# Attention, top-1 experts and a softplus layer on one core: where buffers are zeroed, in how many pieces squares are made, in which order VectorE leaves the attention, and which engine makes the last x

## The chip, the cores and the metric

The program runs on one core of one Trainium2 chip. The metric is the device time of one execution in microseconds (us); the time before is the median of three runs. A profiled execution has a time of its own, and its trace is what the rows below come from. Engines are named as in the profile: PE is TensorE, DVE is VectorE, ACT is ScalarE, POOL is GpSimd, and SP is SyncE, which only issues DMAs here.

## The reference

Three stages follow one another; the output of each is the input of the next.

```python
# 1 attention with random features: 4 batches, 8 heads, 576 positions, 64 wide, 128 features
proj = einsum('bhsd,md->bhsm', x * scale, omega)          # x is q or k
phi = exp(proj - sum(x*x)/2 - max) / sqrt(m)
kv = einsum('bhsm,bhsd->bhmd', k_p, v);  z = k_p.sum(2)
x = einsum('bhsm,bhmd->bhsd', q_p, kv) / (einsum('bhsm,bhm->bhs', q_p, z) + 1e-6)
# 2 top-1 of 8 experts: 2304 tokens, 512 wide, hidden 1024
e = argmax(x @ w_gate);  gate = softmax(x @ w_gate)[e]
x = gate * (relu(x @ w1[e]) @ w2[e])
# 3 a layer for all tokens: 512 -> 2048 -> 512
out = softplus(x @ w_in) @ w_out
```

## The kernel before

**Attention.** It is cut into 20 items. The four batches are two pairs; of each pair five items of k are followed by five of q. An item is two position tiles of 128 of all eight heads (one tile where two rests of 64 rows are put together). So items 0 to 4 are k of the first pair, 5 to 9 its q, 10 to 14 k of the second pair, 15 to 19 its q. One loop runs over n; a step has four slots, and an item passes through it in stages, so that in one step the next item is projected (L510 to L514, each fp32 product in three parts), an item of k is summed up into kv or an item of q is transposed and multiplied (L617, L634), and the item before that is routed. `at(n, slot, ...)` hangs single pieces of work on a slot.

**What each engine does for an item.** POOL makes the sum of squares of the next item in `squares` (L454 the products, L457 the halving sums, then three small ones); DVE takes maxima (L532, L529) and the exponent's bias `nb` (L533); ACT makes the exponentials (L535). For q, DVE makes the reciprocal of the denominator `rc` (L658), the gate logits (L662) and x itself (L666: numerator times reciprocal). The x of an item goes into a tile `xt`, of which there are two in turn, and SP stores it to `x_tok` in memory (L719, L725 where an item is two rests). So the first L666 of an item waits until the store of the item two before it has landed. The two last items, 18 and 19, are the `tail`: their x stays in a tile `own` as well, and is multiplied with the gate by ACT and DVE (L714, L715).

**What lies between.** `clear_y` (L300) lets SP write zeroes, from one tile of SBUF, over a part of `x_tok` (five transfers, 1.0 MB) and over `y_comp` (twenty, 4.7 MB). Experts' weights pass a ring of 16 slots as units: a raw unit is loaded (L237), rounded by ACT (`round_raw`, L247), and DVE keeps the rest (`rest_of_raw`, L252). Units 0, 1 and 4 are loaded while the attention runs. In the passage to the experts, `first_tail` brings the first expert's block together: the gathered rows are multiplied through diagonal matrices that POOL makes (L784, L787), the tail's rows come through one-hot matrices (L767, L770), ACT and DVE split the result (L791, L792), and the first matmuls of the expert (L966 to L968) read it. `places` (from L1103, `key`) works out on DVE where each expert's tokens stand; its first operation takes a buffer whose last users it waits for, among them the stores of `own`.

**What sets the order.** Within an engine the order is the one that a scheduler chooses from its own estimate of times, written code being the preference; `behind(a, b)` fixes that a comes after b. All SP's transfers leave in SP's order, on one queue.

Of the kernel before, what the change touches and what calls it, by code (L numbers as in the profile page):

```python
# [10 lines left out]
F32 = mybir.dt.float32  # L11
# [18 lines left out]
def tile_favor_moe_softplus(  # L30
# [210 lines left out]
            reason="the transfer waits for its turn")  # L241
        return raw

    latest, first_raw = {}, []

    def round_raw(i, raw, last):
        ins = nc.scalar.activation(ring[i % NRING][:, 0:1024], raw, AF.Copy)  # L247
# [41 lines left out]
    with ExitStack() as actx:  # L289
# [157 lines left out]
        def squares(it):  # L447
            src = xin[it.bp, it.kind][it.r // 4][:, :, it.r % 4:it.r % 4 + it.nr, :]
            x2 = wk.tile([P, H, it.nr, D], F32, tag="x2", bufs=1, name="x2")
            if it is items[0]:  # L450
                for h in range(0, H, 4):
                    nc.scalar.activation(x2[:, h:h + 4], src[:, h:h + 4], AF.Square)
            else:
                nc.gpsimd.tensor_tensor(x2, src, src, op=ALU.mult)  # L454
                n = D // 2
                while n:
                    nc.gpsimd.tensor_tensor(x2[:, :, :, 0:n], x2[:, :, :, 0:n], x2[:, :, :, n:2 * n],  # L457
                                            op=ALU.add)
                    n //= 2
                it.sq = sm.tile([P, H, it.nr], F32, tag="sq", bufs=4, name="sq")  # L460
                up = sm.tile([P, H, it.nr], F32, tag="up", bufs=2, name="up")
                whole = x2[:, :, :, 0]
                nc.gpsimd.tensor_scalar(it.sq, whole, 0.5 * SCALE * SCALE, None, op0=ALU.mult)
                nc.gpsimd.tensor_scalar(up, it.sq, LNM, None, op0=ALU.add)
                nc.gpsimd.tensor_tensor(it.sq, up, it.sq, op=ALU.subtract)
            it.x2 = x2
# [157 lines left out]
        def q_product(it, grp):  # L624
# [35 lines left out]
            for g, lo, hi in parts:  # L660
                m = hi - lo
                nc.vector.tensor_tensor(  # L662
                    it.lgp[lo:hi, ii, :, h0:h1].rearrange("p i e h -> p h i e"),
                    cols(g, lo, hi, CG[g], E),
                    rcn[lo:hi].to_broadcast([m, nh, it.nr, E]), op=ALU.mult)
                nc.vector.tensor_tensor(  # L666
                    it.xt[lo:hi, ii, h0:h1, :].rearrange("p i h d -> p h i d"),
                    cols(g, lo, hi, CX[g], D),
                    rcn[lo:hi].to_broadcast([m, nh, it.nr, D]), op=ALU.mult)
# [34 lines left out]
        def route_gate(it):  # L704
            n = it.nr
            ex = sm.tile([P, 2, E], F32, tag="ex", name="ex")[:, 0:n]
            nc.scalar.activation(ex, it.dl, AF.Exp)
            gw = it.xg[:, 0:n, DM]
            nc.vector.tensor_reduce(gw, ex, axis=AX.X, op=ALU.add)
            nc.vector.tensor_scalar(gw, gw, 1e-9, None, op0=ALU.add)  # L710
            nc.vector.reciprocal(gw, gw)
            for i, t in enumerate(it.tiles if it in tail else ()):
                x, g = it.xg[:, i, 0:DM], it.xg[:, i, DM:DM + 1]
                nc.scalar.activation(tail_h[t], x, AF.Copy, scale=g)  # L714
                nc.vector.scalar_tensor_tensor(tail_l[t], x, g, tail_h[t].bitcast(F32),  # L715
                                               op0=ALU.mult, op1=ALU.subtract)
            if n == 2:
                t0 = (2 * it.bp + it.r // 4) * S
                nc.sync.dma_start(  # L719
                    x_tok[t0:t0 + 512, :].rearrange("(p r) d -> p r d", r=4)[  # L720
                        :, it.r % 4:it.r % 4 + 2, :], it.xg)
            else:
                for g in range(2):
                    t0 = (2 * it.bp + g) * S
                    nc.sync.dma_start(x_tok[t0 + 512:t0 + S, :], it.xg[g * 64:(g + 1) * 64, 0, :])  # L725
# [48 lines left out]
        def first_split():  # L774
# [15 lines left out]
            for kk in range(KD):  # L790
                nc.scalar.activation(xh[:, kk, 0:n], tp[kk][:, 0:n], AF.Copy)  # L791
                latest["DVE"] = nc.vector.tensor_tensor(  # L792
                    xl[:, kk, 0:n], tp[kk][:, 0:n], xh[:, kk, 0:n].bitcast(F32), op=ALU.subtract)
            for args in first_raw:
                rest_of_raw(*args)
            return xh, xl

        def route_rank(it):
# [64 lines left out]
        for n in range(NI + 2):  # L863
# [46 lines left out]
                loads(1)  # L910
            if n == 2:
                clear_ids(it.started)
            if n == 12:
                clear_y(it.started)
            if n == 10:
                loads_q(1)
            for i in UNITS_AT.get(n, ()):
                raw = load_raw(i, it.started)
                if i:
                    at(NI, 3, round_raw, i, raw, True)  # L920
                    first_raw.append((i, raw, True))
                else:
                    at(NI - 5, 0, round_raw, i, raw, True)
                    at(NI - 5, 1, rest_of_raw, i, raw, False)
            if n == NI - 2:

                a, b = (inp.tile([P, VO], F32, tag="kf", bufs=2, name="tail") for _ in range(2))
# [172 lines left out]
    def places():  # L1100

        key = tb.tile([P, E], F32, tag="over", name="key")
        nc.vector.scalar_tensor_tensor(key, cntb, float(E), iota_e, op0=ALU.mult,  # L1103
                                       op1=ALU.subtract)

        def rows(a):
            return a.rearrange("p (o e) -> p o e", o=1).to_broadcast([P, R, R])
# [16 lines left out]
        nc.vector.tensor_reduce(cntp[:, 1:E], more, axis=AX.X, op=ALU.add)  # L1124

        off = tb.tile([P, E + 1], F32, tag="off", name="off")
        nc.vector.memset(off[:, E:E + 1], float(NT))
        mc = tb.tile([P, E], F32, tag="nwin", name="mc")
        nc.vector.tensor_tensor(mc, cntp, caps, op=ALU.min)
        for e in reversed(range(E)):  # L1130
# [286 lines left out]
```

## Time and profile before

| | us |
|---|---|
| median of three runs | 845.51 (845.38 to 845.65) |
| the profiled execution | 852.04 |
| its span on the core | 850.3 |
| mean granted clock | 0.991 |
| PE busy | 823.5 |
| DVE, ACT, POOL busy | 490.9, 475.9, 222.5 |

The profiled execution is 6.5 us longer than the median, and 1.7 us of its time lie outside the span. The attention takes the first 185 us or so, the passage lies at 182 to 207 us, the experts and the last layer follow. A strip of the page has 40 slices of 21.3 us each, so that a strip shows in which tenth of the time an engine has gaps; the gaps themselves are read in the order in time.

### The profile page before, as it was taken

The page shows a single profiled execution, that of the slowest core. Times are in us where ns is not written, and L with a number is a line of the kernel's source. Part 1 is how long each engine was busy: PE and PEld are TensorE (multiplying, and loading weights), DVE is VectorE, ACT ScalarE, POOL GpSimd, SP SyncE. Part 2 cuts the span into 40 slices and gives each one's busy share as a digit, 9 for nine tenths or more (in the row PEclk, how much of TensorE's full clock was granted, in tenths as well). Part 3 has the DMA queues.
Part 4 walks back from the last instruction along what each step waited for, and adds up shares of the span by engine and source line. Part 5 has one row for each costly group of instructions (what it writes and reads, how often), then busy time and mean ns, then how long its engine had stood idle before and what let it go on. Part 6 is the DMA issues. An engine that isn't in the chain of part 4 may idle for free.

```text
span 850.3 us, 14078 instructions
## 1 busy us (share of the span) xinstructions
PE 823.5 (97%) x5127; PEld 763.8 (90%) x5129; DVE 490.9 (58%) x1056; ACT 475.9 (56%) x1053; POOL 222.5 (26%) x361
## 2 busy tenths in 40 slices
PE   8998998998999999999999999999999999999995
PEld 6897998987999999999999999999999999999994
DVE  6678976786787677777678666542232223222221
ACT  4686757763564455566555655565455446445442
POOL 6886889223111011101035333211001001001001
PEclk9999998999999999999999999999999999999998
DMA  9962277024896888889853321030001000000001
GB/s 224 225 180 68 72 156 242 26 69 109 263 292 214 267 255 245 278 253 306 277 185 101 124 79 45 1 112 38 1 5 70 1 1 38 1 0 38 1 1 39
DMA packets 83307, 104.21 MB, mean 123 GB/s; under 512 B 16904, under 2 KB 62632, under 8 KB 83234
## 3 DMA queue, kind: packets, MB, share of 16 engines
q1 hardware_dynamic: 79442, 93.35, 36.8%
q0 software_dynamic: 3792, 9.92, 3.5%
q8 instruction: 42, 0.69, 0.4%
q14 instruction: 31, 0.25, 0.1%
HBM read 78.68 MB, written 24.58 MB: 121 GB/s over the span
## 4 chain that ended last, share of the span: by engine, by line
PE 49%; issue 35%; DMA 7%; DVE 3%; POOL 3%; ACT 2%; SPq 1%; POOLq 0%; ACTq 0%; DVEq 0%
PE a L966 6%; PE a L968 6%; PE a L967 6%; PE y L967 4%; PE y L968 4%; PE y L966 4%; PE nm L634 4%; DMA raw<-in_moe_w_dram 2%; PE kvacc L564 2%; PE o L1253 2%; PE o L1251 2%; PE o L1248 2%; POOL out_dram L1268 2%; DMA y_comp<-w 2%; PE tq L617 2%
## 5 line engine op out<-in xcount | busy, mean ns | idle before, releaser
L1236 DVE SCALAR_TENSOR_TENSOR ab<-a,ab 128x384 f32<-128x384 f32 x96 | 53.4, 556 | 161.8 <-ACT ab L1235 151.1
L966 PE MATMUL a<-yh,w 128*128 128x384 f32 x384 | 129.6, 337 | 0.0
L968 PE MATMUL a<-yh,w 128*128 128x384 f32 x384 | 129.5, 337 | 0.0
L967 PE MATMUL a<-yl,w 128*128 128x384 f32 x384 | 129.0, 336 | 0.0
L1253 PE MATMUL o<-w,gl 128*128 128x512 f32 x288 | 114.0, 397 | 0.0
L1251 PE MATMUL o<-w,gh 128*128 128x512 f32 x288 | 113.9, 396 | 0.0
L1248 PE MATMUL o<-w,gh 128*128 128x512 f32 x288 | 112.9, 393 | 0.1
L1233 ACT ACTIVATE ab<-a 128x384 f32<-128x384 f32 x96 | 47.1, 491 | 113.0 <-PE a L968 112.9
L269 DVE TENSOR_TENSOR w<-raw,w 128x1024 fp32r<-128x1024 f32 x69 | 84.2, 1222 | 26.6 <-ACT w L266 25.9
L535 ACT ACTIVATE ph<-pj,nb 128x128 f32<-128x128 f32 x288 | 82.2, 395 | 30.0 <-DVE nb L533 21.0
L266 ACT ACTIVATE w<-raw 128x1024 fp32r<-128x1024 f32 x69 | 72.8, 1057 | 37.6 <-DMA raw<-in_moe_w_dram 37.3
L1268 POOL DMA_INDIRECT out_dram<-ob,idx x18 | 17.6, 976 | 280.7 <-ACT ob L1266 277.2
L1240 DVE TENSOR_TENSOR gl<-ab,gh 128x384 fp32r<-128x384 f32 x96 | 60.6, 631 | 52.1 <-ACT gh L1239 52.1
L1239 ACT ACTIVATE gh<-ab 128x384 fp32r<-128x384 f32 x96 | 50.4, 525 | 54.0 <-DVE ab L1236 53.7
L967 PE MATMUL y<-hl,w 128*128 128x344 f32 (+6 forms) x256 | 78.7, 308 | 0.0
L968 PE MATMUL y<-hh,w 128*128 128x344 f32 (+6 forms) x256 | 78.1, 306 | 0.0
L966 PE MATMUL y<-hh,w 128*128 128x344 f32 (+6 forms) x256 | 75.8, 306 | 1.4 <-ACT hh L1041 1.4
L967 PEld LDWEIGHTS a<-yl,w 128*128 128x128 f32 x384 | 72.4, 189 | 4.2
L966 PEld LDWEIGHTS a<-yh,w 128*128 128x128 f32 x384 | 72.2, 188 | 4.4 <-DVE ab L1236 0.2
L968 PEld LDWEIGHTS a<-yh,w 128*128 128x128 f32 x384 | 72.0, 188 | 0.0
L966 PE MATMUL a<-xh,w 128*128 128x344 f32 (+6 forms) x224 | 69.1, 309 | 0.3 <-DVE hl L1042 0.3
L968 PE MATMUL a<-xh,w 128*128 128x344 f32 (+6 forms) x224 | 67.7, 302 | 0.0
(231 smaller groups left out, 1879.6 us busy)
## 6 DMA issues: line engine op xcount, KB each, us to landing
raw<-in_moe_w_dram SPq DMA_DIRECT2D x64, 512.0 KB
raw<-in_moe_w_in_dram SPq DMA_DIRECT2D x16, 512.0 KB
raw<-in_moe_w_out_dram SPq DMA_DIRECT2D x16, 512.0 KB
yb<-y_comp SPq DMA_DIRECT2D x6, 768.0 KB
vf<-in_v_dram SPq DMA_DIRECT2D x4, 1024.0 KB
qf<-in_q_dram SPq DMA_DIRECT2D x4, 1024.0 KB
y_comp<-w SPq DMA_DIRECT2D x16, 256.0 KB
wi_f<-cvr SPq DMA_DIRECT2D x16, 256.0 KB
```

What stands on the lines that cost most here:

```text
L266: ins = nc.scalar.activation(slot[:, c:c + 1024], raw[:, c:c + 1024], AF.Copy)
L269: nc.vector.tensor_tensor(slot[:, 1024 + c:1024 + c + 1024], raw[:, c:c + 1024], slot[:, c:c + 1024].bitcast(F32), op=ALU.subtract)
L535: ins = nc.scalar.activation(dst[j], pj[:, j // 2, j % 2, :], AF.Exp, bias=nb[:, j // 2, j % 2:j % 2 + 1])
L966: nc.tensor.matmul(o, lhsT=wH, rhs=xH, start=first, stop=False)
L967: nc.tensor.matmul(o, lhsT=wH, rhs=xL, start=False, stop=False)
L968: nc.tensor.matmul(o, lhsT=wL, rhs=xH, start=False, stop=last)
L1236: nc.vector.scalar_tensor_tensor(ab, a, 0.0, ab, op0=ALU.max, op1=ALU.add)
L1239: placed[0] = nc.scalar.activation(gh, ab, AF.Copy)
L1240: placed[1] = nc.vector.tensor_tensor(gl, ab, gh.bitcast(F32), op=ALU.subtract)
L1248: ins = nc.tensor.matmul(os[t], lhsT=gh[:, s], rhs=u[:, c:c + DM], start=f == 0, stop=False)
L1251: nc.tensor.matmul(os[t], lhsT=gh[:, s], rhs=u[:, 1024 + c:1024 + c + DM], start=False, stop=False)
L1253: ins = nc.tensor.matmul(os[t], lhsT=gl[:, s], rhs=u[:, c:c + DM], start=False, stop=f == NF2 - 1)
```

## The change

1. `clear_y` is called in step n == 8 and not in step n == 12: its transfers wait for the last projection of item 8.
2. `squares` on POOL is cut: the products (L454) and the first halving sum (L457) run in two halves of four heads each.
3. Raw unit 0 is rounded two steps later (in step 17 and not 15). The rests of units 1 and 4 come right behind the tail's last L715, ahead of the expert's first split, and no longer behind it.
4. `key` of `places` stands behind the last DVE operation of that split (L792), and the memset of `off` behind `key`.
5. The x of item 19 is made by ACT: 16 activations of 64 x 64 with the reciprocal as scale, in place of six DVE operations.

```diff
-    latest, first_raw = {}, []
+    latest = {}
...
-                nc.gpsimd.tensor_tensor(x2, src, src, op=ALU.mult)
+                for h in range(0, H, 4):
+                    hs = slice(h, h + 4)
+                    nc.gpsimd.tensor_tensor(x2[:, hs], src[:, hs], src[:, hs], op=ALU.mult)
                 n = D // 2
                 while n:
-                    nc.gpsimd.tensor_tensor(x2[:, :, :, 0:n], x2[:, :, :, 0:n], x2[:, :, :, n:2 * n],
-                                            op=ALU.add)
+                    step = 4 if n > D // 4 else H
+                    for h in range(0, H, step):
+                        a = x2[:, h:min(h + step, H)]
+                        nc.gpsimd.tensor_tensor(a[:, :, :, 0:n], a[:, :, :, 0:n],
+                                                a[:, :, :, n:2 * n], op=ALU.add)
                     n //= 2
...
+                if it is items[-1]:
+
+                    for h in range(nh):
+                        nc.scalar.activation(
+                            it.xt[lo:hi, 0, h0 + h, :],
+                            nm[lo:hi, h * DG + CX[g]:h * DG + CX[g] + D], AF.Copy,
+                            scale=rcn[lo:hi, h, 0, :])
+                    continue
...
-                nc.vector.scalar_tensor_tensor(tail_l[t], x, g, tail_h[t].bitcast(F32),
-                                               op0=ALU.mult, op1=ALU.subtract)
+                latest["DVE"] = nc.vector.scalar_tensor_tensor(
+                    tail_l[t], x, g, tail_h[t].bitcast(F32), op0=ALU.mult, op1=ALU.subtract)
...
-            for args in first_raw:
-                rest_of_raw(*args)
...
-            if n == 12:
+            if n == 8:
                 clear_y(it.started)
...
                     at(NI, 3, round_raw, i, raw, True)
-                    first_raw.append((i, raw, True))
+                    at(NI + 1, 3, rest_of_raw, i, raw, True)
                 else:
-                    at(NI - 5, 0, round_raw, i, raw, True)
-                    at(NI - 5, 1, rest_of_raw, i, raw, False)
+                    at(NI - 3, 0, round_raw, i, raw, True)
+                    at(NI - 3, 1, rest_of_raw, i, raw, False)
...
-        nc.vector.scalar_tensor_tensor(key, cntb, float(E), iota_e, op0=ALU.mult,
-                                       op1=ALU.subtract)
+        ins = nc.vector.scalar_tensor_tensor(key, cntb, float(E), iota_e, op0=ALU.mult,
+                                             op1=ALU.subtract)
+        behind(ins, latest["DVE"])
...
-        nc.vector.memset(off[:, E:E + 1], float(NT))
+        behind(nc.vector.memset(off[:, E:E + 1], float(NT)), ins)
```

Before, SP's transfers from the store of item 5 (xt_944) on stand in this order; xt_1115 is item 6, the two of xt_1272 are item 7, xt_1459 and xt_1646 are items 8 and 9.

```order
L719 DMA x_tok_67<-xt_944 128x1026 [waits DMAHW7_49,DVE_49]
L719 DMA x_tok_67<-xt_1115 128x1026 [waits DMAHW0_49,DVE_49]
L368 DMA qf_1718<-in_q_dram 128x8x256 [waits DMAHW1_49,PE_49,Pool_49]
L725 DMA x_tok_67<-xt_1272 64x513 [waits DMAHW2_49,DVE_49]
L725 DMA x_tok_67<-xt_1272 64x513 [waits DMAHW3_49]
L719 DMA x_tok_67<-xt_1459 128x1026 [waits DMAHW4_49,DVE_49]
L719 DMA x_tok_67<-xt_1646 128x1026 [waits DMAHW5_49,DVE_49]
L300 DMA x_tok_67<-w11_80 128x513 [waits DMAHW6_49,PE_49]
...
L237 DMA raw_1970<-in_moe_w1_dram 128x4x256 [waits DMAHW7_49]
L237 DMA raw_2070<-in_moe_w1_dram 128x4x256 [waits DMAHW0_49,PE_49]
```

After, with other numbers for the same tiles, the order of SP is this; xt_958 is item 5, xt_1131 item 6, xt_1290 item 7.

```order
L733 DMA x_tok_67<-xt_958 128x1026 [waits DMAHW7_49,DVE_49]
L300 DMA x_tok_67<-w11_80 128x513 [waits DMAHW0_49,PE_49]
L300 DMA x_tok_67<-w11_80 128x513 [waits DMAHW1_49]
L733 DMA x_tok_67<-xt_1131 128x1026 [waits DMAHW2_49,DVE_49]
L300 DMA y_comp_70<-w11_80 128x512 [waits DMAHW6_49]
...
L739 DMA x_tok_67<-xt_1290 64x513 [waits DMAHW2_49,DVE_49]
L739 DMA x_tok_67<-xt_1290 64x513 [waits DMAHW3_49]
L368 DMA qf_1765<-in_q_dram 128x8x256 [waits DMAHW4_49,PE_49,Pool_49]
L733 DMA x_tok_67<-xt_1504 128x1026 [waits DMAHW5_49,DVE_49]
L733 DMA x_tok_67<-xt_1693 128x1026 [waits DMAHW6_49,DVE_49]
L237 DMA raw_1996<-in_moe_w1_dram 128x4x256 [waits DMAHW7_49,PE_49]
```

The 25 transfers of zeroes were behind the stores of items 5 to 9, right ahead of the raw units; now two of them are ahead of the store of item 6, and all of them ahead of the two stores of item 7.

On DVE, around the first x of item 9 (xt_1646), the order before was this.

```order
L666 TENSOR_TENSOR xt_1646<-nm_1639,rc_1650 128x3x2x64 [waits DMAHW3_49,DMAHW2_49]
L709 TENSOR_REDUCE xt_1459<-ex_1599 128x2 [waits Activation_49]
L710 TENSOR_SCALAR xt_1459<-xt_1459 128x2 [waits DVE_49]
L711 RECIPROCAL xt_1459<-xt_1459 128x2 [waits DVE_49]
L499 SCALAR_TENSOR_TENSOR w15_81<-tp_1678,xT_1683 128x512 [waits Activation_49]
L532 TENSOR_REDUCE mx_1706<-pj_1670 128x4 [waits PE_49]
L655 SCALAR_TENSOR_TENSOR rc_1693<-eps_1648,nm_1686 128x6 [waits PE_49]
L806 TENSOR_TENSOR t1_1631<-rk_1627,oh_1557 128x16 [waits PE_49]
```

After, where xt_1693 is the tile of item 9, L680 the line of x and L538 that of the maximum, it is this.

```order
L820 TENSOR_REDUCE sl_1680<-t1_1678 128x2 [waits DVE_49]
L668 TENSOR_TENSOR lgp_1694<-nm_1733,rc_1740 128x3x16 [waits DVE_49]
L829 CAST si_1682<-sl_1680 128x2 [waits DMASW3_49,DMASW2_49,DVE_49]
L538 TENSOR_REDUCE mx_1753<-pj_1717 128x4 [waits PE_49]
L680 TENSOR_TENSOR xt_1693<-nm_1686,rc_1697 128x3x2x64 [waits DMAHW3_49,DMAHW2_49]
L539 TENSOR_TENSOR nb_1752<-sq_1454,mx_1753 128x4 [waits DVE_49]
L538 TENSOR_REDUCE mx_1775<-pj_1767 128x4 [waits PE_49]
L680 TENSOR_TENSOR xt_1693<-nm_1733,rc_1740 128x3x2x64 [waits DVE_49]
L539 TENSOR_TENSOR nb_1774<-sq_1641,mx_1775 128x4 [waits DVE_49,Pool_49]
```

The first x of item 9 has moved behind the maximum L538, and what stood behind it, the ranks of item 8 among it, now stands ahead of it; the two waits of that instruction are those for the two stores of item 7.

At the end of the passage DVE had this order before; L949 takes the experts' counts, L792 is the split that the first expert's matmuls read.

```order
L715 SCALAR_TENSOR_TENSOR tail_2827<-own_2828,tail_2827 128x512 [waits Activation_49]
L949 COPY cntb_132<-ct_3176 128x8 [waits PE_49]
L1123 COPY cntp_133<-cntb_132 128x1 [waits DVE_49]
L792 TENSOR_TENSOR w15_81<-xtp0_3127,w11_80 128x344 [waits Activation_49]
L1103 SCALAR_TENSOR_TENSOR key_3229<-cntb_132,iota_e_118 128x8 [waits DMAHW0_49,DMASW7_49,DMAHW1_49,DMASW1_49,DMAHW6_49,DMASW0_49,DMAHW7_49,PE_49,Pool_49]
L1127 MEMSET off_3244 128x1
L792 TENSOR_TENSOR w15_81<-xtp1_3128,w11_80 128x344 [waits Activation_49]
L1113 TENSOR_TENSOR more_3231<-key_3229 128x49 [waits DVE_49]
L792 TENSOR_TENSOR w15_81<-xtp2_3129,w11_80 128x344 [waits Activation_49]
L792 TENSOR_TENSOR w15_81<-xtp3_3130,w11_80 128x344 [waits Activation_49]
L252 TENSOR_TENSOR w1_73<-raw_2070,w1_73 128x1024
L252 TENSOR_TENSOR w4_76<-raw_2072,w4_76 128x1024
```

After, where L806 is the split, L961 takes the counts and L1115 is `key`, it has this one.

```order
L729 SCALAR_TENSOR_TENSOR tail_2865<-own_2866,tail_2865 128x512 [waits Activation_49]
L252 TENSOR_TENSOR w1_73<-raw_2098,w1_73 128x1024 [waits DMAHW0_49]
L252 TENSOR_TENSOR w4_76<-raw_2100,w4_76 128x1024 [waits DMAHW1_49]
L961 COPY cntb_132<-ct_3226 128x8 [waits PE_49]
L1136 COPY cntp_133<-cntb_132 128x1 [waits DVE_49]
L806 TENSOR_TENSOR w15_81<-xtp0_3175,w11_80 128x344 [waits Activation_49]
L806 TENSOR_TENSOR w15_81<-xtp1_3176,w11_80 128x344 [waits Activation_49]
L806 TENSOR_TENSOR w15_81<-xtp2_3177,w11_80 128x344 [waits Activation_49]
L806 TENSOR_TENSOR w15_81<-xtp3_3178,w11_80 128x344 [waits Activation_49]
L1115 SCALAR_TENSOR_TENSOR key_3277<-cntb_132,iota_e_118 128x8 [waits DMAHW0_49,DMAHW1_49,DMASW7_49,DMAHW4_49,DMASW1_49,DMAHW7_49,DMASW0_49,Pool_49]
L1140 MEMSET off_3292 128x1
```

The two rests L252 went from behind the four splits to ahead of the counts, and `key`, which was between the first and the second split with its waits, is behind the fourth.

## Rows read from the trace of the kernel before

**Rows 1.** This is the page: busy time of each engine over the span, then the strips of 40 equal slices for TensorE and for the clock that was granted to it.

```profile
PE 823.5 (97%) x5127; PEld 763.8 (90%) x5129; DVE 490.9 (58%) x1056; ACT 475.9 (56%) x1053; POOL 222.5 (26%) x361
...
PE   8998998998999999999999999999999999999995
...
PEclk9999998999999999999999999999999999999998
```

**Rows 2.** This is busy time by engine in six stretches of the span. The columns are the stretch and its length, busy us of each engine with its instructions, the granted clock, the DMA share and GB/s.

```profile
76.00:84.00 8.00, 4.81 (x44) 3.80 (x40) 7.66 (x27) 3.22 (x10) 4.52 (x10) 1.00 0.26 78
84.00:116.00 32.00, 31.45 (x274) 30.76 (x274) 27.72 (x94) 20.43 (x65) 26.25 (x50) 1.00 0.27 86
140.00:143.00 3.00, 1.31 (x8) 0.75 (x7) 2.89 (x3) 2.46 (x9) 3.00 (x3) 0.88 0.13 48
143.00:152.50 9.50, 9.14 (x43) 9.14 (x44) 3.87 (x13) 3.37 (x10) 6.63 (x16) 0.50 0.18 57
182.00:207.00 25.00, 21.12 (x155) 16.46 (x154) 17.63 (x83) 7.76 (x17) 9.60 (x11) 1.00 0.39 93
207.00:850.00 643.00, 633.18 (x3612) 588.26 (x3612) 336.29 (x588) 346.19 (x649) 84.49 (x71) 1.00 0.37 118
```

**Rows 3.** This is the order in time from 139 to 144 us: ScalarE, VectorE and TensorE, one after the other. The columns are start, busy us, engine, line and operation, tiles, shape and count; in brackets the idle time before, and who ended it.

```profile
139.02 1.06 ACT L247 ACTIVATE w<-raw 128x1024 fp32r<-128x1024 f32 x1 [0.72 <-DMA raw<-in_moe_w_dram]
...
140.11 2.44 DVE L252 TENSOR_TENSOR w<-raw,w 128x1024 fp32r<-128x1024 f32 x1 [1.05 <-ACT w L247]
...
141.44 0.55 PE L593 MATMUL kvtp<-ident,kv 128*128 128x128 f32 x3 [1.43 <-ACT ph L535]
143.36 1.01 PE L634 MATMUL nm<-kv,qT 128*128 128x128 f32 x3 [0.61 <-DVE kv L603]
```

**Rows 4.** This is groups of instructions by line, with different shapes kept apart: busy us in all, mean ns of one, idle time before. Then two rows of the order in time, one of VectorE and one of TensorE.

```profile
L454 POOL TENSOR_TENSOR x<-kf 128x1024 f32<-128x1024 f32 x7 | 13.2, 1892 | 5.2 <-DMA kf<-in_k_dram 5.2
...
L454 POOL TENSOR_TENSOR x<-km 128x512 f32<-128x512 f32 x2 | 2.1, 1056 | 0.0
...
L457 POOL TENSOR_TENSOR x<-x 128x512 f32<-128x512 f32 x15 | 19.1, 1276 | 0.1
...
L457 POOL TENSOR_TENSOR x<-x 128x256 f32<-128x256 f32 x19 | 13.9, 730 | 0.9
...
L533 DVE TENSOR_TENSOR nb<-sq,mx 128x4 f32<-128x4 f32 x36 | 16.6, 472 | 1.7 <-POOL sq L465 0.6
...
75.26 1.72 DVE L686 TENSOR_TENSOR dl<-lg,rmx 128x16 f32<-128x16 f32 x1
...
78.49 0.17 PE L801 MATMUL rk<-oh,tri_b 128*128 128x16 bf16 x1 [1.71 <-DVE oh L693]
```

**Rows 5.** This is the order in time of the DMA issues of SyncE around the zeroes, and below it two stretches by busy time and GB/s, columns as in Rows 2.

```profile
114.03 2.46 SPq L300 DMA_DIRECT2D x_tok<-w  x5
116.53 16.25 SPq L300 DMA_DIRECT2D y_comp<-w  x20
132.93 1.21 SPq L237 DMA_DIRECT2D raw<-in_moe_w_dram  x2
...
120.00:124.50 4.50, 4.50 (x42) 4.50 (x41) 4.05 (x7) 3.50 (x12) 4.33 (x6) 1.00 1.03 117
124.50:133.00 8.50, 8.47 (x73) 8.10 (x72) 6.84 (x12) 5.67 (x21) 7.47 (x16) 1.00 1.06 369
```

**Rows 6.** This is the order in time where the zeroes go in the changed kernel: TensorE's last matmul of item 8, VectorE's first x of item 8 and the operation ahead of the x of item 9 in the new order, and SyncE's stores of items 6 and 7.

```profile
85.31 0.28 PE L514 MATMUL pj<-w,w 128*128 128x256 f32 x1
...
88.56 0.55 DVE L666 TENSOR_TENSOR xt<-nm,rc 128x384 f32<-128x384 f32 x1
...
100.32 0.68 DVE L532 TENSOR_REDUCE mx<-pj 128x4 f32<-128x512 f32 x1
...
80.55 0.34 SPq L719 DMA_DIRECT2D x_tok<-xt  x1
90.66 1.15 SPq L725 DMA_DIRECT2D x_tok<-xt  x2
```

**Rows 7.** This is the order in time of the passage between the stages: VectorE, ScalarE, GpSimd, TensorE.

```profile
186.46 0.34 DVE L666 TENSOR_TENSOR own<-nm,rc 64x192 f32<-64x192 f32 x1
...
191.04 0.29 DVE L666 TENSOR_TENSOR own<-nm,rc 64x128 f32<-64x128 f32 x1
...
200.01 0.52 DVE L792 TENSOR_TENSOR w<-xtp,w 128x344 fp32r<-128x344 f32 x1 [3.42 <-ACT w L791]
202.10 0.17 DVE L1103 SCALAR_TENSOR_TENSOR key<-cntb,iota_e 128x8 f32<-128x8 f32 x1 [1.57 <-DMA x_tok<-own]
202.19 0.51 DVE L792 TENSOR_TENSOR w<-xtp,w 128x344 fp32r<-128x344 f32 x1
...
203.59 2.35 DVE L252 TENSOR_TENSOR w<-raw,w 128x1024 fp32r<-128x1024 f32 x2
...
187.12 0.21 ACT L707 ACTIVATE ex<-dl 128x16 f32<-128x16 f32 x1
189.93 1.33 ACT L714 ACTIVATE tail<-own 128x512 fp32r<-128x512 f32 x2 [2.60 <-DVE own L711]
...
193.66 1.71 POOL L784 TENSOR_SCALAR diags<-ident,tail 128x128 f32<-128x128 f32 x3
...
202.76 0.42 PE L967 MATMUL a<-w,w 128*128 128x344 f32 x1 [0.96 <-DVE w L792]
```

## The prediction

> **What bounds the kernel now.** I read the page's busy times and strips first. PE works 823.5 of 850.3 us, and in its strip every slice from the eleventh on (from 213 us) is a 9 [rows 1]. The table by stretches says the same: from 207 us on PE works 633 of 643 us [rows 2]. The change touches nothing there that PE waits for, so it can only move the moment at which the experts get going. Ahead of that the reader should look for PE's gaps and for the clock. 76 to 84 us has 3.2 us of gaps, 140 to 143 us 1.7 us, the passage 182 to 207 us 3.9 us; and from 143 to 152.5 us the granted clock is 0.50, the lower of its two levels (1.2 GHz), while PE is busy 9.14 of 9.5 us [rows 2]. From 84 to 116 us, where the zeroes go, PE works 31.45 of 32 us and DVE 27.7 [rows 2]: two engines near their bound, so what stalls DVE there stalls PE.
>
> Then I read the order in time at the gaps. Ahead of the fall of the clock ACT rounds unit 0 at 139.02 and DVE takes its rest at 140.11 for 2.44 us, in the middle of the passage from k to q; PE idles 1.43 and 0.61 us, the second until DVE's kv [rows 3]. The other reader's view is the groups with shapes apart: a square of 1024 elements on POOL takes 1.89 us, and DVE's `nb`, an operation of 128 x 4, takes 472 ns in the mean. A single `dl` of 128 x 16 at 75.26 took 1.72 us, and 1.71 us is what PE then waited for `oh` behind it [rows 4]. Small DVE operations last as long as a POOL operation that runs beside them.
>
> **The zeroes, step by step.** This is the largest term, and it is a loss. SP's issues of zeroes begin at 114.03, and what is behind them is issued at 132.93: 18.9 us for 25 transfers, 5.8 MB [rows 5]. One stretch of it ran at 117 GB/s, another at 369 [rows 5]. After, the block begins when item 8's last projection ends, Z = 85.31 + 0.28 = 85.6 [rows 6]. In the order shown, the store of item 6 stands behind two of the zeroes, and both stores of item 7 behind all of them; before, they left at 80.55 and 90.66 [rows 6]. The x of item 8 waits for the store of item 6: DVE is there at 88.56, 3.0 us after Z; the data ahead and of its own (1.0 MB) take 2.8 us at 369 GB/s, and a landing of 2.2 to 4.7 us (the upper end from the raw unit below, 6.1 us less 1.4 for its own 0.5 MB; the lower an estimate of half of it) gives Z + 5 to 7.5, a first stall of 2 to 4.5 us. The x of item 9 waits for item 7. It stands behind L532, which ended at 100.32 + 0.68 = 101.0 [rows 6]. The store is issued at Z + 18.9 + 1.4 (item 6's own 0.5 MB) = 105.9; for the landing I take the raw unit of before, issued at 132.93 [rows 5] and there for ACT at 139.02 [rows 3], 6.1 us. That gives 112.0. The first stall doesn't add, since the second ends at a fixed time. **DVE is late by 112.0 - 101.0 = 11.0 us, and PE with it.** Bounds: 4.1 us if all 6.6 MB go at 369 GB/s (17.8 us, and an estimated 1.7 us to land, a third of the 4.7 above: 105.1), 13 us if the slow stretch is some 2 us longer. I take 11, since the same transfers with the same source showed the slow stretch.
>
> What PE does in these stalls matters too. In the first, PE idles longer than it did at 140 us, so the clock may fall there as it did at 142 [rows 2, 3]; the half clock then fills time that PE would have waited in the second stall, and costs nothing of its own. I leave a second fall out of the sum and price it as a rival.
>
> **The other parts.** (a) The clock at 143 us: unit 0 moves two items on and no longer meets the passage from k to q. 9.14 us of PE's work at 0.50 would need 4.6 at full clock [rows 2]; 4.2 gained, since some waits for DVE don't shrink. (b) The two waits ahead, 1.43 and 0.61 us [rows 3]: 1.4 gained, as the kv passage has waits of its own. (c) The unit goes among q items where PE has no gaps to give: between 0 and 1.2 us (half of DVE's 2.35 for two [rows 7]), 0.4 lost. (d) Halves: POOL's operations fall from 1892 to 1056 ns and from 1276 to 730 [rows 4], so the longest time that DVE is held falls by 0.84 us, and POOL works 2 x 1056 - 1892 + 2 x 730 - 1276 = 0.40 us longer per item, which is hidden where POOL isn't waited for: `nb` waited for POOL 0.6 us in the whole run [rows 4]. `nb` has 472 ns where some 165 would be free: 36 x 0.3 = 11 us of DVE, halved to 5.5, of which PE sees what falls into its gaps. I take 1.9 ahead of Z (1.2 of the 3.2 us at 76 to 84, where one lock was worth 1.71 [rows 4], and 0.7 at the start), and 1.0 behind it; bounds 0.5 and 5. (e) The passage: `key` waited for the store of `own` until 202.10 between two splits, and PE's `a` idled 0.96 us for the second split at 202.19 [rows 7]. With `key` behind all four this goes. The two L252 (2.35 us) go into the 3.42 us in which DVE waits for ACT's split ahead of 200.01 [rows 7]; cover gone, they would push it. (f) The last x: DVE loses six operations of 0.3 us between 186.46 and 191.04 [rows 7], ACT gains 16 small ones, at the nearest row, 0.21 us of L707, 3.4 us, beside an idle time of 2.60 [rows 7]; between -1 and +1 us for the tail's L714, zero taken. POOL's three diagonals (from 193.66 [rows 7]) now come partly behind an indirect transfer; 0.2 lost. (e) and (f) together gain 0.8, bounds -1 and 1.5.
>
> **Sum.** Lost: 11.0 + 0.4 = 11.4. Gained: 4.2 + 1.4 + 1.9 + 1.0 + 0.8 = 9.3. Net 2.1 us: the profiled execution's 852.04 would be 854.1. The profiled execution lies 6.5 us above the median, 4.2 to 4.6 us of which could be the very fall of the clock; the trace can't tell whether the timed runs have it. I assume they do and transfer the difference: 845.5 + 2.1 = 847.6.
>
> **A rule against the sum.** The rows show these 2 KB rows at 117 GB/s for 4.5 us and at 369 for 8.5 us [rows 5]. The Trainium skill, page "DMA: Bandwidth & Descriptors", section Specifications, says that transfers of 512 B or more go at line rate, with a limit of about 358 GB/s for a core's memory. By that page 6.6 MB take 18.4 us, item 7 lands near Z + 20, and the result is the first rival's. The trace agrees in the second stretch and differs in the first.
>
> **The rivals.** *First, faster: the zeroes run through at full rate.* The slow stretch of before came with other traffic or by place, and at Z the queues are quiet (86 GB/s from 84 to 116 us [rows 2]). DVE is then late by 4.1, not 11.0: 847.6 - 6.9 = 840.7; with a fall of the clock less hidden, 841.5. For it: 369 GB/s from 124.5 on [rows 5]. Against it: the slow stretch began with just the x_tok zeroes that come first again. *Second, slower still: the clock falls after the second stall,* as it fell after shorter gaps at 142 us [rows 3]: another 9 us at 0.50, 847.6 + 4.2 = 851.8. It decides once PE idles some us in that stall although it was slowed before it; against it, 3.2 us of gaps at 76 to 84 us left the clock at 1.00 [rows 2]. The same 851.8 comes out if the fall at 142 us was not in the timed runs, since (a) is then worth nothing. *Third, no change: the parts don't do what they say.* The stall is some 9 us, the passage gains nothing because ACT's 16 operations hold L714 and L252 holds the first split, and gains and losses cancel: 845.5, within 1.7. *A fourth, below 839,* would need that no stall reaches PE (836); 1 in 50, counted with the first.
>
> **How the numbers follow.** 0.2% is 1.7 us, about what a measurement of this kernel can tell from no change. Likeliest (845.9 to 849.6): 0.34, of it 0.06 within 0.2%. First rival (839.0 to 843.5): 0.32. Second (850 to 854.5): 0.20. Third: 0.14, of it 0.10 within, 0.02 on either side. Faster 0.32 + 0.02 = 0.34; same 0.06 + 0.10 = 0.16; slower 0.28 + 0.20 + 0.02 = 0.50. The range from 839.5 to 853.5 leaves out the ends of the two outer cases. Cases of both signs hold most of the chance; the likeliest one's own range is 845.9 to 849.6.
>
> **What would show it.** In the trace after: a DVE x write (L680) that waits for a DMA at about Z + 3 and a second one until about Z + 26, with PE idle behind it; if that wait ends by Z + 20, the first rival is right. The clock strip should be without the fall at 142 us, or show it at 90 to 125 us. In the passage no `key` between the splits and no 0.96 us ahead of `a`. POOL's rows should read 1.06 and 0.73 us, with `nb` below 350 ns. The prediction is wrong if DVE meets no DMA wait there, or if PE has work enough in hand to pass over it.

## The result, and the profile after

The changed kernel takes 856.44 us in the median of four runs (855.14 to 857.08), beside 845.44 us for the kernel before timed beside it: a ratio of 1.013 [1.0113, 1.0148], 11.0 us slower. Run once more beside other kernels it came to 1.0122 [1.0086, 1.0159]. The forecast of 847.6 us had the direction; the time lies above its range. One execution of a run below (e12, 1148.88 us at a granted clock of 0.655) was a slow one and is left out of its time and its ratio.

The first page rows answer to [rows 1]; after TensorE's row stands the clock that it was granted.

```profile
span 853.4 us, 14130 instructions
...
PE   8999879998999999999999999999999999999995
...
PEclk9999989998999999999999999999999999999998
```

The fall of the clock in the seventh slice (142 us) is gone, and there are new ones, in the sixth slice (107 to 128 us) and the tenth (192 to 213 us); the table by stretches, in the columns of [rows 2], tells where. It also has one that the strip doesn't show, in its first row.

```profile
78.00:81.40 3.40, 3.40 (x20) 2.94 (x20) 3.22 (x13) 0.60 (x1) 2.58 (x7) 0.50 0.34 128
84.00:103.50 19.50, 18.45 (x162) 17.89 (x161) 13.98 (x58) 13.17 (x40) 16.00 (x34) 1.00 1.04 260
103.50:112.00 8.50, 0.42 (x4) 0.24 (x3) 0.52 (x2) 0.00 (x0) 4.59 (x11) 0.81 0.97 197
112.00:116.00 4.00, 3.91 (x19) 3.67 (x19) 3.97 (x15) 3.79 (x13) 0.00 (x0) 0.56 0.26 103
116.00:182.00 66.00, 65.27 (x573) 64.37 (x573) 49.03 (x153) 50.56 (x162) 46.55 (x98) 1.00 0.21 57
182.00:205.00 23.00, 21.31 (x161) 17.41 (x160) 16.86 (x79) 10.91 (x32) 10.59 (x11) 1.00 0.51 115
205.00:209.00 4.00, 0.49 (x3) 0.31 (x2) 1.70 (x10) 0.82 (x2) 0.00 (x0) 0.84 0.60 97
209.00:215.00 6.00, 6.00 (x23) 6.00 (x23) 5.22 (x13) 4.14 (x6) 1.83 (x2) 0.54 0.76 231
```

Two holes stand out: from 103.5 to 112 us TensorE does next to nothing, and from 205 to 209 us again; behind each the clock is at its lower level (1.2 GHz) for some us. The fall at 78 us stands where the prediction found 3.2 us of gaps and a clock of 1.00. It is not in every execution: another trace of the changed kernel (f4 below) has a clock of 1.00 there.

```profile
78.00:81.40 3.40, 3.28 (x31) 2.83 (x30) 3.22 (x14) 0.60 (x1) 2.67 (x7) 1.00 0.51 176
```

The order in time of SyncE's issues, and then of VectorE and TensorE, shows what the first one is; it answers to [rows 5, 6].

```profile
79.37 0.82 SPq L300 DMA_DIRECT2D x_tok<-w  x2
80.28 0.41 SPq L733 DMA_DIRECT2D x_tok<-xt  x1
80.74 2.64 SPq L300 DMA_DIRECT2D x_tok<-w  x3
83.42 18.54 SPq L300 DMA_DIRECT2D y_comp<-w  x20
102.50 1.09 SPq L739 DMA_DIRECT2D x_tok<-xt  x2
...
88.91 0.56 DVE L680 TENSOR_TENSOR xt<-nm,rc 128x384 f32<-128x384 f32 x1 [0.97 <-DMA x_tok<-xt]
...
111.48 0.56 DVE L680 TENSOR_TENSOR xt<-nm,rc 128x384 f32<-128x384 f32 x1 [10.21 <-DMA x_tok<-xt]
...
112.09 0.59 PE L561 MATMUL kvacc<-zero_b 128*128 128x512 bf16 x1 [8.17 <-DVE xt L680]
```

The x of item 9 waits 10.21 us for the store of item 7, which SyncE issued only behind the twenty y_comp zeroes, and TensorE waits 8.17 us for VectorE. The last rows are of the passage, from ScalarE's, SyncE's, GpSimd's, VectorE's and TensorE's order in time; they answer to [rows 7].

```profile
190.71 1.85 ACT L675 ACTIVATE own<-nm,rc 64x64 f32<-64x64 f32 x8
...
208.18 0.46 ACT L1053 ACTIVATE hh<-a 128x344 fp32r<-128x344 f32 x1 [6.29 <-DMA id_slot<-tok,si]
...
197.37 7.16 SPq L260 DMA_DIRECT2D raw<-in_moe_w_dram  x2
...
199.60 1.02 POOL L831 DMA_INDIRECT id_slot<-tok,si  x1 [0.17 <-issue]
...
200.88 1.78 DVE L806 TENSOR_TENSOR w<-xtp,w 128x344 fp32r<-128x344 f32 x4 [2.14 <-ACT w L805]
204.26 0.17 DVE L1115 SCALAR_TENSOR_TENSOR key<-cntb,iota_e 128x8 f32<-128x8 f32 x1 [1.60 <-DMA x_tok<-own]
...
208.69 1.51 PE L978 MATMUL y<-hh,w 128*128 128x344 f32 x4 [3.51 <-ACT hh L1053]
```

The four splits do run in a row and the 0.96 us ahead of `a` are gone, as forecast. But the first hh now waits until 208.18 for GpSimd's last scatter, issued at 199.60 behind a raw load of 197.37 and landed at 207.62, and TensorE waits 3.51 us for hh. In the trace of before that wait was 1.39 us, and in that of e1 (below) 0.35 us; the row of before:

```profile
206.94 0.89 PE L966 MATMUL y<-hh,w 128*128 128x344 f32 x4 [1.39 <-ACT hh L1041]
```

### The profile page after: what moved, and what is told of

Its sections match the earlier page's. It is cut to its first block, busy times and chain, and to the rows that moved or that the text cites. A ratio compares the mean times of both kernels' runs of the same rounds, so it can differ in the third digit from the quotient of the medians.

```text
span 853.4 us, 14130 instructions
## 1 busy us (share of the span) xinstructions
PE 821.9 (96%) x5128; PEld 764.9 (90%) x5129; DVE 482.8 (57%) x1050; ACT 479.7 (56%) x1069; POOL 230.3 (27%) x399
## 4 chain that ended last, share of the span: by engine, by line
PE 53%; issue 34%; DMA 5%; POOL 3%; DVE 2%; ACT 1%; SPq 1%; POOLq 0%; ACTq 0%; DVEq 0%
PE a L978 7%; PE a L980 6%; PE a L979 6%; PE y L978 4%; PE y L979 4%; PE y L980 4%; PE kvacc L570 4%; PE nm L640 3%; PE o L1266 2%; PE o L1264 2%; PE o L1261 2%; POOL out_dram L1281 2%; PE pj L516 1%; PE pj L519 1%; PE pj L520 1%
## 5 line engine op out<-in xcount | busy, mean ns | idle before, releaser
L978 PE MATMUL a<-yh,w 128*128 128x384 f32 x384 | 129.6, 337 | 0.0
L269 DVE TENSOR_TENSOR w<-raw,w 128x1024 fp32r<-128x1024 f32 x69 | 84.3, 1221 | 19.4 <-ACT w L266 19.1
L978 PE MATMUL y<-hh,w 128*128 128x344 f32 (+6 forms) x256 | 77.1, 309 | 3.5 <-ACT hh L1053 3.5
L980 PE MATMUL y<-hh,w 128*128 128x344 f32 (+6 forms) x256 | 78.6, 307 | 0.0
L978 PEld LDWEIGHTS a<-yh,w 128*128 128x128 f32 x384 | 72.2, 188 | 4.4 <-DVE ab L1249 0.2
L1053 ACT ACTIVATE hh<-a 128x344 fp32r<-128x344 f32 (+6 forms) x64 | 27.3, 426 | 75.4 <-PE a L980 64.1
L978 PE MATMUL a<-xh,w 128*128 128x344 f32 (+6 forms) x224 | 69.1, 308 | 0.0
```

What stands on the lines that cost most here:

```text
L269: nc.vector.tensor_tensor(slot[:, 1024 + c:1024 + c + 1024], raw[:, c:c + 1024], slot[:, c:c + 1024].bitcast(F32), op=ALU.subtract)
L978: nc.tensor.matmul(o, lhsT=wH, rhs=xH, start=first, stop=False)
L980: nc.tensor.matmul(o, lhsT=wL, rhs=xH, start=False, stop=last)
```

## The experiments

All edits are against the changed kernel unless it says otherwise; "passage" is the time from the start of the last row of nm (L640, L634 before) to the first y (L978, L966). Ratios are against the kernel before.

**The kernel before, again (e1_before).** No edit.

> The kernel before, unchanged, to see which execution its median stands for. Theory A (the profiled execution of before was an odd one: its clock fell at 142 us, that of the timed runs did not): most executions have a granted clock near 0.996 and spans near 843.7 us, and a trace of one shows no fall at 142 us and no 1.4 us gap of TensorE there. Rival (the fall is in every execution, and 6.5 us are what recording costs): clock 0.991 in all, the fall at 142 us again, spans that are 1.7 us below the times.

0.9994 [0.9982, 1.0006], spans of 841.2 to 844.5 us, granted clocks of 0.992 to 0.998. The trace has no fall of the clock at 142 us; its strip:

```profile
PEclk9999999999999999999999999999999999999998
```

Of 105 further runs of the kernel before that were timed beside these kernels (25, 34, 33 and 13) two took over 850 us (851.62 and 853.05, clocks 0.986 and 0.988); where their clock fell is not on record. So the execution that the prediction was made from was a rare one, and theory A holds: the fall of the clock was hardly ever there to be gained. The shorter gaps were: TensorE is busy 28.33 of 30 us from 120 to 150 us in this trace.

**Zeroes at n == 12 (e2_after_z12), at n == 9 (e5_after_z9), and at n == 8 on the kernel before (e3_before_z8).**

```diff
-            if n == 8:
+            if n == 12:        # e2; n == 9 in e5; e3 is before.py with n == 8
                 clear_y(it.started)
```

> The changed kernel with clear_y called at n == 12 again, all else of the change kept. Theory A (nearly the whole loss is VectorE's wait for the store of item 7 behind the zeroes, 8.2 us of TensorE idle and 1.9 us of half clock, and the other parts are worth little): 845 to 847 us, about 10 us below the changed kernel. Rival B (the passage has become worse by itself, TensorE waiting 3.5 us for hh and then at half clock): 850 us or more. Rival C (the other parts gain what the prediction gave them): 838 to 841 us.

> The changed kernel with clear_y at n == 9: the same transfers one item later, now behind the stores of item 6 and all but three of them behind item 7's, so that no x waits for all of them. Theory A: no long wait of VectorE for a store, within 2 us of the run with n == 12, 844 to 848 us. Rival D (it is the 5.8 MB moving beside the attention that slow VectorE and TensorE, not the order in the queue): 852 us or more, as with n == 8.

> The kernel before with clear_y called at n == 8, nothing else changed. Theory A: VectorE waits for the stores of items 6 and 7 as in the changed kernel, 855 to 858 us. Rival B (the passage makes the loss): 846 to 850 us, since the passage is that of the kernel before.

e2: 0.9984 [0.9974, 0.9993], 843.85 us, between theory A's range and rival C's. e5: 0.9989 [0.9978, 1.0001], 844.37 us, with no wait of an x for a store. e3: 1.0085 [1.0051, 1.0118], 851.38 us, between its two sides, with a wait of 5.71 us for item 7. One step later in the loop gives back 1.4%, 12 us, with the same bytes beside the attention. The zeroes on the kernel before cost 0.85%, not the 10 us that theory A said: the wait is shorter in its trace, and something else of the change adds to it.

**The two stores of item 7 off SyncE's queue (e11_z8_pool_store).** Zeroes stay at n == 8.

```diff
+                    eng = nc.gpsimd if it is items[7] else nc.sync
-                    nc.sync.dma_start(x_tok[t0 + 512:t0 + S, :], ...)
+                    eng.dma_start(x_tok[t0 + 512:t0 + S, :], ...)
```

> The changed kernel as it is, zeroes at n == 8 and all its orders, but GpSimd issues the two stores of item 7, so that they don't stand behind the zeroes on SyncE's queue. VectorE keeps its order and its wait for these stores. Theory A (place in the queue is the whole of the loss): the wait of 10.2 us ahead of item 9's x is gone or under 1 us, TensorE's 8.2 us of idle time too, 844 to 846 us. Rival D (the 5.8 MB beside the attention make stores land late on any queue): the wait stays above 5 us, 850 us or more.

1.0020 [1.0000, 1.0041], 847.19 us, between the two sides. GpSimd issues them while SyncE is still at the zeroes, and the x of item 9 doesn't wait (orders in time of GpSimd, VectorE and TensorE):

```profile
93.51 1.17 POOL L740 DMA_DIRECT2D x_tok<-xt  x2
...
105.20 0.55 DVE L680 TENSOR_TENSOR xt<-nm,rc 128x384 f32<-128x384 f32 x1
...
105.80 0.38 PE L561 MATMUL kvacc<-zero_b 128*128 128x512 bf16 x1 [0.31 <-DVE xt L680]
```

VectorE's order did not stay wholly as it was. In the changed kernel this x stands right behind a maximum that ends at 101.27; here the scheduler put other operations between them, so that it starts at 105.20 and not at 101.68, where the maximum ends. It would not have waited there either: the two stores landed at 99.51 and 99.86 us. The place in the queue is worth 1.10%, 9.3 us. Most of it lies ahead of the issue: the later of the two stores lands 11.5 us earlier than in the changed kernel (99.86 against 111.38), and it is issued 9.0 us earlier. The Trainium skill, page "DMA: Bandwidth & Descriptors", section "Queues, rings and completion order", has each DMA engine take its queues in turn and each queue in its order; these two runs agree, since behind the zeroes on SyncE's queue the stores are issued at 102.5 us, and on the other at 93.5, with the zeroes still being issued.

**The passage at n == 9: x of item 19 back on VectorE (e6), VectorE's old last order (e7), both (e8).**

```diff
-                if it is items[-1]:              # e6, e8
+                if False:
-                    at(NI + 1, 3, rest_of_raw, i, raw, True)      # e7, e8
+                    first_raw.append((i, raw, True))     # called behind the splits
-        behind(ins, latest["DVE"])
```

> The changed kernel with clear_y at n == 9 and the last x made by VectorE again (its part 5 undone); beside 844.4 us with part 5. From the last nm of L640 to the first y the passage took 20.6 us there, and 18.4 in the kernel before. Theory P (the 16 small operations on ScalarE hold L728 and what follows, so part 5 is what makes the passage longer): passage 18.5 to 19.5 us, 842 to 843 us. Rival Q (the early rests L252 and their raw loads ahead of the last scatters are what makes it longer): no change in time, 844 to 845 us, passage 20 us or more.

> The changed kernel with clear_y at n == 9 and the old order on VectorE at the end (rests of units 1 and 4 behind the split, key where the scheduler puts it). Theory P: passage stays above 20 us, 844 to 845 us. Rival Q: 18.5 to 19.5 us and 842 to 843 us.

> The changed kernel with clear_y at n == 9 and both the last x and VectorE's last order as before, so that only zeroes, halves and unit 0 differ from the kernel before. Theory (the attention is 5 us shorter by halves and unit 0, and the passage is then that of the kernel before): last nm near 178.5 us, passage 18.4, 840 to 841 us, below both kernels. Rival R (the passage is longer because the attention ends earlier than the scatters and stores that it waits for): passage above 20 us again, 843 to 845 us.

e6: 0.9976 [0.9965, 0.9987], passage 20.5 us. e7: 0.9981 [0.9967, 0.9994], passage 19.4. e8: 0.9960 [0.9947, 0.9974], 841.44 us, passage 18.5, where e5 has 20.6. Neither P nor Q alone: together the two parts cost 0.29%, 2.4 us, each some 1 us (their intervals overlap). About 1 us of e5's loss lies behind the first y and was not taken apart.

In e6 hh waits 3.09 us of TensorE's time, and as in the changed kernel it is for the last scatter: GpSimd issues it at 186.76, SyncE a raw load at 186.82, and the scatter takes 9.0 us to land. (The profile names the raw load as what hh waits for; the load of that name lands only at 196.96, when hh has begun.) The order in time of GpSimd and SyncE, the landing, and TensorE:

```profile
186.76 1.97 POOL L831 DMA_INDIRECT id_slot<-tok,si  x1 [0.30 <-DVE w L252]
...
186.82 5.23 SPq L260 DMA_DIRECT2D raw<-in_moe_w_dram  x2
...
id_slot<-tok,si POOLq DMA_INDIRECT x1, 9.0
...
196.72 1.51 PE L978 MATMUL y<-hh,w 128*128 128x344 f32 x4 [3.09 <-ACT hh L1053]
```

In e7 the wait is at `key`, between two splits again, for a store of `own`:

```profile
192.39 0.17 DVE L1117 SCALAR_TENSOR_TENSOR key<-cntb,iota_e 128x8 f32<-128x8 f32 x1 [2.38 <-DMA x_tok<-own]
```

In e5 the wait is a third one, seen in VectorE's and TensorE's order in time:

```profile
184.24 0.17 PE L815 MATMUL rk<-base_b,ones_b 128*128 128x8 bf16 x1
...
187.80 0.17 DVE L818 TENSOR_TENSOR t<-rk,oh 128x8 f32<-128x8 f32 x1 [3.40 <-remote]
...
188.74 0.87 PE L781 MATMUL xtp<-tail 128*128 128x344 f32 x4 [2.95 <-DVE si L829]
```

VectorE waits for rk 3.40 us longer than TensorE's rows say it takes, and the last one-hot matrix and TensorE's next matmuls come late by it.

**Whole squares at n == 9 (e9), and halves with unit 0 at its old place (e10).** e10 is e8 with unit 0's two calls at NI - 5.

```diff
-                for h in range(0, H, 4): ...      # e9
+                nc.gpsimd.tensor_tensor(x2, src, src, op=ALU.mult)
-                    step = 4 if n > D // 4 else H
+                    step = H
```

> The changed kernel with clear_y at n == 9 and whole squares (part 2 undone). Theory (halves are what shortens the attention): last nm at 182 us or later in place of 178.4, 847 to 849 us. Rival S (unit 0's place shortens it, and halves do nothing): no change, 844 to 845 us.

> The run with clear_y at n == 9 and the old passage (841.4 us), with unit 0 rounded at its old place as well, so that against the kernel before only halves and the zeroes' step differ. Theory (unit 0's place gave the median little, since most executions had no fall of the clock at 142 us): within 1.5 us of 841.4, 841 to 843 us. Rival (the place of unit 0 was worth the 5.6 us that the prediction gave it): 845 to 847 us, with the fall of the clock near 140 us in the trace.

e9: 1.0013 [0.9999, 1.0026], 846.0 us, between its two sides, last nm at 181.66 against 178.40 us in e5; halves give 0.24%, 2.0 us, not by much clear of the noise, since the intervals of e9 and e5 touch. The groups of the changed kernel show how, against [rows 4]:

```profile
L463 POOL TENSOR_TENSOR x<-x 128x256 f32<-128x256 f32 x45 | 32.3, 732 | 0.8
...
L457 POOL TENSOR_TENSOR x<-kf 128x512 f32<-128x512 f32 x14 | 14.3, 1038 | 4.0 <-DMA kf<-in_k_dram 3.9
L539 DVE TENSOR_TENSOR nb<-sq,mx 128x4 f32<-128x4 f32 x36 | 10.2, 300 | 1.2 <-POOL sq L471 0.5
```

`nb` takes 300 ns where it took 472 in the trace of before and 377 in e1. With nothing but the squares different, e9 and then e5:

```profile
L537 DVE TENSOR_TENSOR nb<-sq,mx 128x4 f32<-128x4 f32 x36 | 17.2, 491 | 1.1
```

```profile
L539 DVE TENSOR_TENSOR nb<-sq,mx 128x4 f32<-128x4 f32 x36 | 10.5, 304 | 1.7 <-POOL sq L471 0.9
```

The Trainium skill, page "SBUF — State Buffer", section "SBUF: two separate sides", calls the port pair of VectorE and GpSimd a lock that is held for a whole instruction; a shorter hold with shorter instructions agrees with it. e10: 1.0005 [0.9982, 1.0027], against 0.9960 with unit 0 moved. The rival's time came, without the fall of the clock that was its reason. So unit 0's place is worth 0.45%, 3.8 us: the stretch from 120 to 150 us in e10, then in e8.

```profile
120.00:150.00 30.00, 26.43 (x223) 25.22 (x222) 20.49 (x46) 22.49 (x72) 27.27 (x56) 1.00 0.18 57
```

```profile
120.00:150.00 30.00, 29.79 (x264) 29.55 (x262) 21.83 (x52) 24.97 (x81) 27.27 (x55) 1.00 0.14 42
```

TensorE loses 3.57 us there with unit 0 in the passage from k to q, and 0.21 with it two items on. In e10 halves alone gained nothing, so the 2.0 and the 3.8 us each hold with the other part in place and need not add up.

**Zeroes at n == 8 and 12 with the old passage (e12, e13).** e8 with another n.

> The run with clear_y at n == 9 and the old passage (841.4 us), with clear_y at n == 8. Theory (the wait in the attention costs 11 us whatever the passage is): 851.5 to 853 us. Rival (part of the 12 us comes from the changed passage, which after the late attention waits for a scatter and meets the half clock): 846 to 850 us.

> Halves and unit 0's place alone on the kernel before, zeroes at n == 12. Theory (the zeroes cost the same at 9 and 12, as with the changed passage, where 844.4 stood beside 843.9): 840.5 to 842 us. Rival (zeroes at 12 hold raw units and slow the passage from k to q): 843 us or more.

e12: 1.0051 [1.0032, 1.0071], 850.01 us; its wait for item 7 is 7.21 us. e13: 0.9944 [0.9925, 0.9963], 841.14 us, the best kernel of all, below both. In e12 neither side was right in full: from e8 the zeroes' step costs 0.91%, 7.7 us, where with the changed passage it costs 1.4%.

**What of the passage adds to the wait (f1, f2), the loss without both (f3), and the changed kernel again (f4).** f1 and f2 are e7 and e6 with n == 8; f3 is e12 with e11's edit.

> The changed kernel, zeroes at n == 8, with VectorE's old order at the end alone (rests of units 1 and 4 behind the split, key free). Theory T (the early rests let SyncE load the next unit ahead of the last scatter, hh then waits 3.5 us for that scatter and TensorE falls to half clock): the wait of hh for the scatter is gone and the time is 850 to 852 us. Rival U (the last x on ScalarE makes it, since its lateness puts the last scatter behind): hh still waits, 854 us or more.

> The changed kernel, zeroes at n == 8, with the last x on VectorE alone. Theory T: hh still waits for a transfer behind the split, 854 us or more. Rival U: the wait is gone, 850 to 852 us.

> Zeroes at n == 8, halves, unit 0's new place, the old passage, and the two stores of item 7 issued by GpSimd. If the loss of the changed kernel is the place in the queue and the passage and nothing else: no wait for item 7, 841 to 843 us, as with the zeroes at 9 or 12. Rival (zeroes at n == 8 slow the attention by their traffic as well): 845 us or more.

> The changed kernel itself, beside the others. 855 to 857 us with a granted clock of 0.985 to 0.987 in all executions if the wait in the attention and the half clock in the passage belong to it; if the passage's fall of the clock was of one execution alone, some executions should be near 852 us with a clock above 0.99.

f1: 1.0081 [1.0049, 1.0112]. f2: 1.0089 [1.0061, 1.0116]. Beside f4 either edit gives back some 3 us by the medians, but their intervals overlap with f4's. f4: 1.0122, runs of 853.07 to 858.72 us, two of the four below the range expected, with clocks of 0.990 and 0.991; in its trace hh doesn't wait for long, and VectorE waits 3.33 us for rk.

Theory T is right about what makes hh wait, though not about the times. hh waits for the scatter with the early rests alone (f2, 2.70 us of TensorE's time, the scatter landing 8.5 us after its issue) and not with the last x on ScalarE alone (f1, landing in 4.7 us). The traces side by side say more: where the early rests let SyncE load the next unit just when the last scatter is issued or ahead of it (the changed kernel, e6, e9, f2), that scatter took 7.2 to 9.0 us to land, and where the load left later, 4.0 to 5.4 us. One trace is against a plain cause: before, 7.9 us with no such load.

f1 has the late rk instead (VectorE waits 3.33 us). So in each trace with the early rests, the last x on ScalarE, or both, TensorE waits at one of three places: for hh behind the scatter, behind the late rk, or behind `key` (e7). With both old (e1, e3, e8, e10, e12, e13, f3) no wait of TensorE's in the passage is over some 1.2 us; only the trace of before has the 1.39 us.

f3: 0.9975 [0.9962, 0.9988], 843.71 us: without queue place and passage the zeroes at 8 still cost 1.3 us against e8 and 2.6 us against e13. That is not clear of the noise: f3's interval overlaps with both of theirs.

## Why the prediction was wrong

From the kernel before to the changed one there is a way in single steps, and it can be laid beside the sum, in per cent of 845.4 us; an estimate from the intervals of the ratios gives each step an uncertainty of 0.2 to 0.3 points:

| step | runs | measured | forecast |
|---|---|---|---|
| halves and unit 0's place ((a) to (d)) | before to e13 | -0.56%, -4.7 us | -8.1 us |
| zeroes at 8, item 7's stores off the queue | e13 to f3 | +0.31%, +2.6 us | 0 |
| passage ((e), (f)) | f3 to e11 | +0.45%, +3.8 us | -0.8 us |
| item 7's stores behind the zeroes | e11 to changed | +1.10%, +9.3 us | +11.0 us |
| sum | | +1.30%, +11.0 us | +2.1 us |

**The stall was right in place and mechanism.** The store of item 7 was there at 111.4 us, 112.0 was forecast. That it fits to 0.6 us is luck, since two errors cancel: the block began at 79.37 and not at 85.6, because it waits for an earlier projection than I read, and it took 23.1 us to item 7's store and 8.9 to land, not 20.3 and 6.1. The first rival, zeroes at full rate, did not come: from 84 to 103.5 us the memory moved 260 GB/s, not 369. The first stall was 0.97 us, under its bound of 2. The second rival's fall of the clock came (0.56 in the mean from 112 to 116 us); it is within the 9.3.

**The step that failed first: "(e) and (f) together gain 0.8, bounds -1 and 1.5".** They lose: 2.4 us with the zeroes at 9 (e5 against e8), 3.8 here. What (e) set out to remove, `key` and the wait ahead of `a`, is gone, and the cover for the two L252 held: behind them VectorE still idles 2.14 us for ScalarE's split. What the term lacks is what the end of L252 sets free: I named the queue behind it on VectorE and not the raw load on SyncE that leaves at that moment, beside the last scatter that hh waits for. "Zero taken" for ScalarE's 16 operations seems to have failed too: with them alone 0.2% is lost (e7 against e8, with intervals that overlap), and the trace has its wait behind `key`.

**The second: "(a) ... 4.2 gained", and with it "I assume they do and transfer the difference".** The fall of the clock was in the recorded execution and at most in 2 of some 105 timed ones. The third part of the second rival said so, at 851.8 us. Yet unit 0's place was worth 3.8 us by the gaps alone, where (a) to (c) had 5.2; halves gave 2.0 where (d) had 2.9, each with the other in place. So of a gain of 8.1 us 4.7 were there (e13).

**The third** is a term that the sum may lack: zeroes at 8 cost 2.6 us, or 1.3 against e8, without any wait for a store. It is not clear of the noise, and whether it is traffic or order is not settled.

Some readings of the prediction are off without changing a case: TensorE's strip ends in a 5 and not in a 9, a third of 4.7 is 1.6, and 847.6 less 11.0 is 836.6.

**What stays open.** Whether the wait is dearer with the changed passage, 9.3 us (e11 to changed) against 6.4 (f3 to e12), is not shown: the two overlap within their uncertainty, and the waits seen were 10.21 and 8.63 us in two traces of the changed kernel against 7.21. Why the last scatter lands late beside a raw load, and in the trace of before without one, is open. So is why VectorE's wait for rk ends 3.1 to 3.4 us after TensorE's rows for it, in e2, e5, e11, f1 and f4. All of these have ScalarE making the last x, but so have the changed kernel, e7 and e9, whose traces don't show it; no run took it apart.

## What to carry to other kernels

A transfer that only fills memory isn't free because it is early: look at which small stores get behind it on the same queue, and who waits for their buffers; one step of the loop was worth 8 to 12 us here, and another queue for those stores 6 to 9 us. Price the passage by what each moved instruction sets free, its transfers included, not by the idle time that it fills. And where one profiled execution is longer than the timed runs, take a second trace before a gain is read from what is only in the first.

## What the hardware showed that was not expected

The same zeroes from the same tile took 18.9 us at n == 12 and 23.1 us at n == 8 (one store of 0.5 MB among them) to the next issue behind them, and the two stores of 128 KB behind them 8.9 us to land. And a matmul whose row ends at 184.41 released its reader at 187.80.
